# Transposing DMAs for the second LayerNorm's rows, and a lead of three jobs, in a one-core transformer block

## The chip, the cores and the metric

The kernel runs on one core of a Trainium2 chip. A core has a matrix engine (PE), which multiplies into PSUM (eight banks of 512 fp32 columns), a vector engine (DVE), a scalar engine for activations (ACT), a general engine (POOL), and a sync engine (SP), which here issues every DMA. The engines run independent instruction streams and wait for each other by semaphores. The time is device microseconds of one execution; a result is the median over several.

## What is computed

One pre-LayerNorm block on 2048 rows of 1024 bf16 values, with 32 heads of 32 and an FFN of width 3584:

```
x  = A_x
qkv = layernorm(x) @ wqkv
p   = softmax(q k^T * 32**-0.5)          # per head, all 2048 keys, no mask
h   = x + (p v) @ wo
h2  = h + gelu(layernorm(h) @ w1 + b1) @ w2 + b2     # gelu in its tanh form
```

## The kernel before, in words

**Work units.** Rows are cut into 8 units of 256 rows (`UNITS`, line 463), heads into G = 8 groups of 4. A job (unit, group) takes 8 rounds, each of two chunks of 128 keys. A round (`Att.qk`, line 926) is 8 small score matmuls into four PSUM banks (two of the three pairs in banks 0 to 5) and two exps on ACT of 128x1024 each into a slot of the ring PT (9 slots; line 952). `Job.pv` (line 988) multiplies the exps by V and adds up the softmax's denominators: usually DVE adds the round's two chunks into PS (line 1013), for QUAD jobs also two such sums into one (line 1019), and PE multiplies the sums by ones (`den`, line 1029, matmuls at line 1036). The last round of a job is summed "directly" by PE from PT, without DVE. 64 jobs make 1024 exps. `finish` (line 1044) divides and writes OT.

**The lead** (lines 1252 to 1304). Rows are loaded in tiles of 128 (`x_tile`) with slices of the QKV weights (`load_w`), normalized on DVE with a power on POOL (`layer_norm`, line 717; statistics at line 715, the normalization at line 741), transposed by PE through PSUM (line 763), and copied to xnT by ACT (line 770; the ten tiles of `LEAD_ACT`) or DVE (line 772). For each half-chunk hc of 256 rows, `proj_half` (line 898) makes K and, for hc 0 and 1, Q of group 0. As K arrives, rounds of the jobs (0, 0) and (1, 0) start; the exps of the first lie in PT, those of the second in eight buffers PX that overlay K and V of later groups. V of group 0 (`proj_v1`, line 885) follows, then the PVs of the lead's jobs.

**After the lead.** `ORDER` (line 1280) lists first the jobs (2, 0) and (3, 0), then units 0 and 1 for the groups 1 to 7, with the projections of each group just ahead. Q for later units is projected later (`late_q`) by way of a scratch in HBM. From there on, unit by unit: `wo` (line 1099) adds the attention's projection to x, giving hch; `ln2` (line 1139) normalizes hch into xb, and for every unit but the last calls `transposes` (line 760): eight PE transposes into one background bank and one DVE copy into hnT. `ffn1` (line 1162) reads hnT; its first matmul waits for the FFN2 of the unit before. `gelu` runs on DVE with a tanh on ACT (line 1215), and `ffn2` (line 1229) ends the unit. All of this fills PE between the scores and PVs of the attention of units 2 to 7. The last unit's wo, LayerNorm and FFN (`tail=True`) come after all attention and use all banks; its transposes use `transposes_2`.

**What sets the order.** Every operation is a task of a graph (`Graph.add`, line 85) with the buffers it reads and writes, an estimated cost and a priority. `Graph.schedule` (line 110) simulates the engines with these estimates: when an engine comes free, DVE, ACT, POOL and SP take the ready task of least priority number, PE what `pick_pe` (line 1417) chooses among scores, PV, denominators and background work. The order found is written out as fixed instruction streams, so on the chip every engine works strictly in that order. A DMA is modelled as 1.6 us, plus bytes at 340 GB/s, plus 1.0 us, 0.42 us apart on SP, and the large ones (512 KB and over) are also paced. The tables `PV_BEGIN`, `PV_MUST`, `GROUP_SHIFT` and `PRIO_SHIFT` shift that order by numbers found by search. Background matmul groups use banks 6 and 7 only, as does each job's PV.

Of the kernel before, what the change touches and what calls it, by code (L numbers as in the profile page):

```python
# [12 lines left out]
P = 128  # L13
BF = dt.bfloat16
F32 = dt.float32
# [46 lines left out]
class Graph:  # L62
# [47 lines left out]
    def schedule(self, pick_pe, pool, switch=(0.11, 0.106, 0.1), dma_rate=340.0, dma_first=1.6, dma_tail=1.0, dma_issue=0.42,  # L110
# [32 lines left out]
        while n < total:  # L143
# [5 lines left out]
            for e in self.ENGS:  # L149
                while free[e] <= now + 1e-9:  # L150
# [6 lines left out]
                    if e == E.SP and now < state["pace"] - 1e-9:  # L157
                        rs = [x for x in rd if x.bytes < pace_bytes]
                        t = min(rs, key=lambda x: (x.prio, num[x]), default=None)
                        heapq.heappush(events, state["pace"])  # L160
                    elif e == E.PE:
                        t = pick_pe(rd, now, state, free_banks(now))
                    else:
                        t = min(rd, key=lambda x: (x.prio, num[x]))
                        if up and t.prio > 0:

                            for (rt, _, u) in up[:6]:
                                if u.prio < t.prio and rt < now + 0.6 * t.occ:
                                    t = None
                                    break  # L170
# [159 lines left out]
    def emit(self, e, obj):  # L330
# [10 lines left out]
PV_BEGIN = "6887668783765478677666734877585674766834855865775635885656674536"  # L341
PV_MUST = "2563656375427345237632753323452322425663763553734473555222232667"
GROUP_SHIFT = (
# [14 lines left out]
PRIO_SHIFT = (  # L358
# [91 lines left out]
def build_kernel(nc, A_x, A_wqkv, A_wo, B_w1, B_b1, B_w2, B_b2, out):  # L450
# [91 lines left out]

    NS = 3
    ot_lo = Area(top.cur)
    PS, B_PS = sb(top, "PS", [P, NS, 4, 256], BF, NS)
    NOT = 2 * G + 2
    OT, B_OT = sb(top, "OT", [P, NOT, 256], BF, NOT, 2)

# [985 lines left out]
```

## Time and profile before

| | |
|---|---|
| runs | 1078.71, 1082.22 and 5466.11 us; median 1082.22 |
| profiled execution | 1079.89 us |
| its span, first to last instruction | 1078.0 us |
| DMA | 173.93 MB; q1 busy 53.1% of 16 engines' span |
| exps to PT (line 952) | 1008, 937.4 us busy |
| PE transposes for hnT (line 763) | 112, 8.8 us busy |
| DVE copies to hnT (line 772) | 14, 9.4 us busy |
| PS additions (lines 1013, 1019) | 439 in 297.4 us; 191 in 130.8 us |

The first page of the profile gives busy time per engine. PEld is PE's loading of weights beside its matmuls. The rows of tenths cut the span into 40 slices of 27 us; 9 is 90% busy or more. A wait row reads: engine, tile and line that waited, what it waited for, then us in total, times, longest us. A windows row gives a stretch, its length, each engine's busy us (instructions), the granted PE clock, the DMA share and GB/s. A timeline row gives start, length, engine, line, operation, output<-input with shapes; lengths overlap a little, so the pitch from start to start is what an instruction costs its engine. A row of DMA issues ends with its count, KB each and the median us from issue to landing.

### The profile page before, as it was taken

How to read it: one execution, taken by the hardware profiler on the slowest of the kernel's cores; microseconds unless marked ns; L12 is line 12 of the kernel's file. 1: busy time of each engine (PE TensorE's matmuls, PEld its weight loads, DVE VectorE, ACT ScalarE, POOL GpSimd, SP SyncE). 2: the span in 40 equal slices, each digit the busy share in tenths (PEclk: the TensorE clock that was granted, in tenths of full speed). 3: DMA queues.
4: the chain of work that ended last, by engine and by line, in shares of the span. 5: the costliest groups of instructions: out<-in, count | busy, mean ns of one | idle time of the engine just before them, and what ended most of it. 6: DMA issues, size and time to landing. Idle time of an engine off the chain costs nothing.

```text
span 1078.0 us, 38343 instructions
## 1 busy us (share of the span) xinstructions
PE 1037.0 (96%) x17162; PEld 586.8 (54%) x17162; DVE 887.6 (82%) x1737; ACT 1016.2 (94%) x1121; POOL 18.8 (2%) x35
## 2 busy tenths in 40 slices
PE   7889999999999999999999999999999999999998
PEld 5546555554446645654466457456645644564483
DVE  8888677777789997998789979988997997997711
ACT  4999999999999999999999999999999999999850
POOL 2000000000000000000000000000000000000000
DMA  7910010005656575754686667558575755987640
GB/s 196 256 60 3 13 49 2 2 2 175 205 153 204 149 224 167 220 164 132 222 259 183 189 197 203 163 173 260 150 222 184 210 150 162 290 258 236 192 153 20
DMA packets 265492, 173.93 MB, mean 161 GB/s; under 512 B 26864, under 2 KB 259952, under 8 KB 264944
## 3 DMA queue, kind: packets, MB, share of 16 engines
q1 hardware_dynamic: 265328, 171.48, 53.1%
q8 instruction: 135, 2.21, 0.8%
q14 instruction: 29, 0.24, 0.1%
HBM read 161.09 MB, written 10.35 MB: 159 GB/s over the span
## 4 chain that ended last, share of the span: by engine, by line
ACT 85%; PE 10%; DVE 3%; DMA 2%; issue 0%; SPq 0%; DVEq 0%
ACT PT L952 79%; PE ps L672 5%; ACT tg L1215 4%; PE ps L669 3%; ACT PX L952 1%; PE ps L941 1%; DMA a_w1r<-in_B_w_dram 1%; DVE st L715 1%; ACT xnT L770 1%; DMA xrb<-in_A_x_dram 0%; PE ps L996 0%; DVE PS L1013 0%; DMA a_w1r<-in_A_wo_dram 0%; DVE xb L741 0%; DVE gT L1192 0%
## 5 line engine op out<-in xcount | busy, mean ns | idle before, releaser
L952 ACT ACTIVATE PT<-ps 128x1024 bf16<-128x1024 f32 x1008 | 937.4, 1148 | 5.4 <-PE ps L941 5.2
L1013 DVE TENSOR_TENSOR PS<-PT 128x1024 bf16<-128x1024 bf16 x439 | 297.4, 684 | 78.1 <-ACT PT L952 52.1
L941 PE MATMUL ps<-QT,KT 32*128 32x256 bf16 x4096 | 203.6, 273 | 13.6 <-ACT PT L952 9.9
L996 PE MATMUL ps<-PT,V 128*32 128x256 bf16 x4032 | 160.5, 273 | 2.9 <-DVE gT L1192 1.1
L941 PEld LDWEIGHTS ps<-QT,KT 32*128 32x128 bf16 x4096 | 60.8, 92 | 170.0 <-ACT PT L952 157.8
L669 PE MATMUL ps<-hnT,a_w1r 128*128 128x256 bf16 x1197 | 148.1, 273 | 1.8 <-DMA a_w1r<-in_B_w_dram 0.7
L1019 DVE TENSOR_TENSOR PS<-PS 128x1024 bf16<-128x1024 bf16 x191 | 130.8, 685 | 3.4
L669 PE MATMUL ps<-a_w2r,gT 128*128 128x512 bf16 x510 | 125.7, 380 | 3.7 <-DVE hnT L772 1.2
L669 PEld LDWEIGHTS ps<-hnT,a_w1r 128*128 128x128 bf16 x1197 | 109.2, 98 | 35.3 <-issue 20.3
L996 PEld LDWEIGHTS ps<-PT,V 128*32 128x32 bf16 x4032 | 100.9, 96 | 37.5 <-issue 6.3
L666 PE MATMUL ps<-a_w2r,gT 128*32 128x512 bf16 x1096 | 80.2, 382 | 0.4 <-DVE gT L1192 0.2
L669 PEld LDWEIGHTS ps<-a_w2r,gT 128*128 128x128 bf16 x510 | 43.8, 98 | 61.9 <-issue 15.0
L1036 PE MATMUL ps<-PS,ones 128*32 128x256 bf16 x1020 | 70.5, 274 | 0.8 <-DVE PS L1013 0.5
L1192 DVE TENSOR_TENSOR gT<-ps,b1f 128x512 bf16<-128x512 f32 x98 | 66.7, 684 | 4.8 <-PE ps L669 2.4
L666 PE MATMUL ps<-hnT,a_w1r 128*32 128x256 bf16 x1484 | 54.5, 274 | 1.7 <-DMA a_w1r<-in_B_w_dram 0.6
L1215 ACT ACTIVATE tg<-tg 128x1024 bf16<-128x1024 bf16 x49 | 55.6, 1148 | 0.0
L669 PE MATMUL ps<-xnT,Wall 128*128 128x512 bf16 (+1 forms) x241 | 51.9, 345 | 2.5 <-ACT xnT L770 1.6
L669 PE MATMUL ps<-Wall,xnT 128*128 128x256 bf16 x345 | 45.6, 274 | 1.4 <-DVE KT L819 0.8
L666 PEld LDWEIGHTS ps<-hnT,a_w1r 128*32 128x32 bf16 x1484 | 36.3, 96 | 13.4 <-issue 11.2
L666 PE MATMUL ps<-xnT,Wall 128*32 128x512 bf16 x540 | 39.1, 381 | 0.6 <-DVE KT L819 0.6
L1244 DVE SCALAR_TENSOR_TENSOR b_ost<-ps,hch 128x512 bf16<-128x512 f32 x4 | 2.8, 692 | 44.7 <-PE ps L672 44.7
L669 PEld LDWEIGHTS ps<-Wall,xnT 128*128 128x128 bf16 x345 | 31.2, 98 | 12.7 <-issue 5.1
(101 smaller groups left out, 998.0 us busy)
## 6 DMA issues: line engine op xcount, KB each, us to landing
a_w2r<-in_B_w_dram SPq DMA_DIRECT2D x105, 512.0 KB, 4.8
a_w1r<-in_B_w_dram SPq DMA_DIRECT2D x98, 512.0 KB, 4.8
a_w1r<-in_A_wo_dram SPq DMA_DIRECT2D x32, 512.0 KB, 4.5
b_w1r<-in_B_w_dram SPq DMA_DIRECT2D x14, 512.0 KB, 5.0
a_w1r<-in_A_wqkv_dram SPq DMA_DIRECT2D x11, 512.0 KB, 4.0
xrb<-in_A_x_dram SPq DMA_DIRECT2D x16, 256.0 KB, 4.1
Wall<-in_A_wqkv_dram SPq DMA_DIRECT2D x16, 256.0 KB, 4.6
hch<-in_A_x_dram SPq DMA_DIRECT2D x16, 256.0 KB, 4.4
```

The source lines that it names most:

```text
L666: fns.append(lambda p, j=j: p.matmul(psum[32 * j:32 * j + 32, bi(bank), c0:c1], lhsT[:, 32 * j:32 * j + 32], rhs, start=start, stop=stop, ...
L669: t.whole = lambda p: p.matmul(psum[:, bi(bank), c0:c1], lhsT, rhs, start=start, stop=stop, skip_group_check=True)
L672: t = pe(lambda p: p.matmul(psum[:, bi(bank), c0:c1], lhsT, rhs, start=start, stop=stop), occ, reads=reads, writes=[bb(bank)], mode="full" ...
L715: return dve(lambda v: v.bn_stats(st_l[:, i, 6 * c:6 * c + 6], src), 0.6, reads=[B_src], writes=[B_stl[i][c]], prio=prio)
L941: return p.matmul(psum[:, 2 * us[h // 2] + h % 2, n * i:n * i + n], KT[32 * h:32 * h + 32, g, k0:k0 + P], QT[32 * h:32 * h + 32, qs, 0:n], ...
L952: act(lambda a, u=u, k=k: a.activation(pt(s)[:, k, :, :], psum[:, 2 * u:2 * u + 2, :], ACT.Exp, bias=0.0, scale=SCALE), 1024, reads=[B_ps[ ...
L996: fns.append(lambda p, i=i, h=h: p.matmul(psum[32 * h:32 * h + 32, bi(bank), 0:nq], V[:, g, nk * r + i, 32 * h:32 * h + 32], pt(s)[:, h // ...
L1013: dve(lambda v: v.tensor_tensor(PS[:, n, :, :], pairs[:, :, 0:256], pairs[:, :, 256:512], ALU.add), c_dve(1024, 2), reads=[B_PT[2 * s], B_ ...
L1019: dve(lambda v: v.tensor_tensor(PS[:, n, :, :], PS[:, n, :, :], PS[:, m, :, :], ALU.add), c_dve(1024, 2), reads=[B_PS[n], B_PS[m]], writes ...
L1036: fns.append(lambda p, h=h, rhs=rhs, i=i: p.matmul(psum[32 * h:32 * h + 32, bi(bank), nq:2 * nq], ones32[:, :], rhs, start=False, stop=las ...
L1192: drop(dve(lambda v: v.tensor_tensor(gT[:, fc:fc + 2, cs], psum[:, bi(bank), 0:2 * n].rearrange("p (f c) -> p f c", f=2), b1f[:, fc:fc + 2 ...
L1215: act(lambda a: a.activation(t, t, ACT.Tanh, bias=0.0, scale=math.sqrt(2.0 / math.pi)), c, reads=B_t, writes=B_t, prio=-1)
```

## The change

The text of the kernel changes in five places, and the four tables and the two costs of PE's mode switches in the planner are replaced.

1. **Second LayerNorm.** `ln2`, for all units but the last, no longer calls `transposes`; it issues one transposing DMA per tile on SP, from xb to hnT, both in SBUF. The planner charges it as 500000 bytes (it moves 262144), below the size that is paced.
2. **Lead.** It holds three whole jobs, (0, 0), (1, 0) and (2, 0). PX grows from 8 to 14 buffers. The first tile is loaded in two halves; K comes before Q in each half-chunk; K, and Q of the first half-chunk, are projected in pieces of 128 rows; the first Q, K and tiles 0 to 3 use fixed banks; tiles 0 to 3 are normalized one by one at higher priority, and until 16 us of planned time DVE may hold back for a more urgent task that is about to be ready. `LEAD_ACT` keeps tiles 0 to 3. The first V eviction, and K and Q of half-chunk 1, go to ACT. Warm-up matmuls go from 50 to 34.
3. **Sums.** The three lead jobs sum all their rounds directly on PE (`DIRECT` 16). `QA` 6: units 6 and 7 no longer make the second DVE addition.
4. **Order of jobs.** (3, 0), then units 0 to 3 for group 1, units 0 and 1 for groups 2 to 4, then unit 0 for groups 5 to 7 and unit 1 for them. OT gets two more slots.
5. **Planner's costs of weight slices** of 128 columns: 2.4 bytes per element in place of 2, and 3.9 for the first ones.

```diff
-                        if up and t.prio > 0:
+                        if up and (t.prio > 0 or e == E.DVE and now < LEAD_HOLD):
...
-                                if u.prio < t.prio and rt < now + 0.6 * t.occ:
+                                if u.prio < t.prio and rt < now + (0.6 if t.prio > 0 else 0.4) * t.occ:
...
-    for k in range(8):
-        lo = att_lo + 2 * S * (k + 2 if k < 6 else G + k - 2)
+    px_at = [att_lo + 2 * S * a for g in range(1, 5) for a in (g, G + g)] + [att_lo + 2 * S * a for a in (5, 6, 7, G + 5)]
+    px_at += [top.cur + 2 * D * 4, top.cur + 2 * D * 6]
+    for k, lo in enumerate(px_at):
...
-    def dma(out_ap, in_ap, nbytes, reads=(), writes=(), prio=0, noncontig=False, after=()):
+    def dma(out_ap, in_ap, nbytes, reads=(), writes=(), prio=0, noncontig=False, after=(), flip=False):
         def fn(s):
+            if flip:
+                return s.dma_start_transpose(out_ap, in_ap)
...
-    N_WARM = 50
-    LEAD_ACT = [0, 1, 2, 3, 4, 6, 8, 10, 12, 14]
+    N_WARM = 34
+    LEAD_ACT = [0, 1, 2, 3]
...
-    QA = 8
+    QA = 6
...
     def DIRECT(qb, g):
-        return 0 if qb < DA else 1
+        return 16 if g == 0 and qb < DLEAD else 1
...
             else:
-                transposes(R.xb[s][:, :], R.B_xb[s], slot(), hnT[:, :, t * P:(t + 1) * P], B_hnT[t], "dve", 0)
+                dma(hnT[:, :, t * P:(t + 1) * P], R.xb[s][:, :], 500000, reads=[R.B_xb[s]], writes=B_hnT[t], prio=-1, flip=True)
...
-    x_tile(0, -6)
+    x_tile(0, -6, 2)
+    x_tile(1, -6)
     load_w(WQ, -5, 0, P)
-    x_tile(1, -5)
+    x_tile(2, -5)
     load_w(WK, -5, 0, P)
-    x_tile(2, -5)
-    x_tile(3, -5)
-    for tt in range(4, 8):
+    for tt in range(3, 8):
         x_tile(tt, -5)
...
-            tr_tile(tt, slot(), "act" if tt in LEAD_ACT else "dve", ev_prio=-4)
-            if tt + 8 < NT:
-                last_x.append(x_tile(tt + 8, -4))
+            tr_tile(tt, 4 + tt % 2 if hc < LEAD_45 else slot(), "act" if tt in LEAD_ACT else "dve", ev_prio=-4)
+            if hc < 4:
+                last_x.append(x_tile(tt + (12 if hc < 2 else 4), -4))
...
-    ORDER = [(2, 0), (3, 0)] + [(k, g) for g in range(1, G) for k in range(2)]
+    ORDER = [(3, 0)] + [(k, g) for g in range(1, G - LATE) for k in (range(4) if g < NEX else range(2))]
+    ORDER += [(k, g) for k in range(2) for g in range(G - LATE, G)]
...
-        for k, r in {0: [(0, 0)], 1: [(0, 1), (1, 0), (1, 1)]}.get(hc, [(0, hc), (1, hc)]):
-            lead.append((k, r, att.qk((k, 0), r, NR + r if k else None)))
+        for k, r in {0: [(0, 0)], 1: [(0, 1), (1, 0), (1, 1)], 2: [(0, 2), (1, 2), (2, 0), (2, 1), (2, 2)]}.get(hc, [(0, hc), (1, hc), (2, hc)]):
+            if (k, r) != (2, 7):
+                lead[k, r] = att.qk((k, 0), r, None if k == 0 else NR + r if k == 1 else NR + 8 + r if r < 6 else NR - 1)
...
     for hc in range(8):
-        proj_v1(2 * hc, 0, 2, slot(), "dve")
+        proj_v1(2 * hc, 0, 2, slot(), "act" if hc < V_ACT else "dve")
...
-    for k in range(2):
+    for k in range(3):
         job = Job(k, 0, slot(2))
-        for k_, r, s in lead:
-            if k_ == k:
-                job.pv(r, s)
+        for r in range(job.nr):
+            job.pv(r, lead[k, r])
+        if k == 0:
+            lead[2, 7] = att.qk((2, 0), 7)
...
-    gr.schedule(pick_pe, pool_banks, (0.114476, 0.110146, 0.1))
+    gr.schedule(pick_pe, pool_banks, (0.115349, 0.111367, 0.1))
```

The new constants are LEAD_HOLD = 16.0, LEAD_45 = 2, LATE = 3, DLEAD = 3, NEX = 2 and V_ACT = 1.

More of the change, by code (lines that the diff above doesn't have):

```diff
@@ L14 @@
 BF = dt.bfloat16
+LEAD_HOLD = 16.0
+LEAD_45 = 2
+LATE = 3
+DLEAD = 3
+NEX = 2
+V_ACT = 1
 F32 = dt.float32
@@ L338, in emit @@
                 ins.then_inc(self.sems[t.flow], 16 if e == E.SP else 1)
-PV_BEGIN = "6887668783765478677666734877585674766834855865775635885656674536"
-PV_MUST = "2563656375427345237632753323452322425663763553734473555222232667"
+PV_BEGIN = "7577886548677765858856674434636846646566545566645345783555878553"
+PV_MUST = "4534436267554436543436636337557333354424733246352322524333334446"
 GROUP_SHIFT = (
[14 rows of a table removed]
-PRIO_SHIFT = (
[85 rows of a table removed]
[12 rows of a table added]
+PRIO_SHIFT = (
[73 rows of a table added]
 def table(s):
@@ L531, in build_kernel @@
     pt_hi = top.cur
+    NS = 3
     PX, B_PX = [], []
-    for k in range(8):
-        lo = att_lo + 2 * S * (k + 2 if k < 6 else G + k - 2)
+    px_at = [att_lo + 2 * S * a for g in range(1, 5) for a in (g, G + g)] + [att_lo + 2 * S * a for a in (5, 6, 7, G + 5)]
+    px_at += [top.cur + 2 * D * 4, top.cur + 2 * D * 6]
+    for k, lo in enumerate(px_at):
         h_, b_ = sb(Area(lo), "PX%d" % k, [P, 2, 2, 512], BF, 2)
@@ L541, in pt @@
         return PT[:, s, :, :, :] if s < NR else PX[s - NR][:, :, :, :]
-    NS = 3
     ot_lo = Area(top.cur)
+    assert top.cur == px_at[-1] - 2 * D * 6
     PS, B_PS = sb(top, "PS", [P, NS, 4, 256], BF, NS)
-    NOT = 2 * G + 2
+    NOT = 2 * G + 2 * NEX
     OT, B_OT = sb(top, "OT", [P, NOT, 256], BF, NOT, 2)
     def ot(u, g):
-        return 2 * G + u - 2 if g == 0 and u in (2, 3) else u % 2 * G + g
+        return 2 * G + 2 * g + u - 2 if g < NEX and u in (2, 3) else 2 * g + u % 2
     xrb, B_xrb_ = sb(ot_lo, "xrb", [P, 8, D], BF, 16)
@@ L780, in load_w, with x_tile @@
         dma(Wall[:, wp(blk), :, c0:c1], A_wqkv[:, blk * 512 + c0:blk * 512 + c1].rearrange("(dc p) c -> p dc c", p=P),
-            P * DC * (c1 - c0) * 2, writes=B_W[wp(blk)][c0 // P:c1 // P], prio=prio, after=after)
+            P * DC * (c1 - c0) * (2 if c1 - c0 > P else 3.9 if prio == -5 else 2.4), writes=B_W[wp(blk)][c0 // P:c1 // P], prio=prio, after=after)
     def x_slot(tt):
-        return xrb[:, tt % 8, :], B_xrb[tt % 8]
-    def x_tile(tt, prio):
+        i = tt if tt < 8 else tt % 8 ^ 4
+        return xrb[:, i, :], B_xrb[i]
+    def x_tile(tt, prio, parts=1):
         ap, b = x_slot(tt)
-        return dma(ap, x2[tt * P:(tt + 1) * P, :], P * D * 2, writes=b, prio=prio)
+        n = D // parts
+        for i in range(parts):
+            t = dma(ap[:, n * i:n * i + n], x2[tt * P:(tt + 1) * P, n * i:n * i + n], P * n * 2,
+                    writes=b if parts == 1 else [b[i]], prio=prio)
+        return t
     def ln_tiles(tts, prio, norm, quick=True):
         layer_norm([x_slot(tt) + (xb[:, tt % NXB, :], B_xb[tt % NXB]) for tt in tts], prio, norm, quick)
-    N_WARM = 50
-    LEAD_ACT = [0, 1, 2, 3, 4, 6, 8, 10, 12, 14]
+    N_WARM = 34
+    LEAD_ACT = [0, 1, 2, 3]
     def tr_tile(tt, bank, evac, prio=0, ev_prio=0):
@@ L889, in proj_v1 @@
             for dc in range(DC):
-                mm(bank, xnT[:, tc, dc, t4 * P:(t4 + 1) * P], Wall[:, wp(4), dc, P * g:P * g + P], dc == 0, dc == DC - 1,
-                   [B_W[wp(4)][g], B_xnTt[tc][t4]], False, cols=(P * k, P * k + P))
+                m = mm(bank, xnT[:, tc, dc, t4 * P:(t4 + 1) * P], Wall[:, wp(4), dc, P * g:P * g + P], dc == 0, dc == DC - 1,
+                   [B_W[wp(4)][g], B_xnTt[tc][t4]] + ([B_xnTt[tc][i] for i in range(t4, t4 + n)] if k == 0 and dc == 0 else []), False,
+                   cols=(P * k, P * k + P), after=lead_end if g == 1 and k == 0 and dc == 0 else ())
         dst = V[:, g, tt:tt + n, :]
         wr = [B_V[NT * g + tt + k] for k in range(n)]
-        t = dve(lambda v: v.tensor_copy(dst, psum[:, bi(bank), 0:P * n].rearrange("p (t c) -> p t c", t=n)), c_dve_ps(P * n),
-                reads=[bb(bank)], writes=wr, prio=-4 if g == 0 else 0)
+        if evac == "act":
+            t = act(lambda a: a.activation(dst, psum[:, bi(bank), 0:P * n].rearrange("p (t c) -> p t c", t=n), ACT.Copy), P * n,
+                    reads=[bb(bank)], writes=wr, prio=-1)
+        else:
+            t = dve(lambda v: v.tensor_copy(dst, psum[:, bi(bank), 0:P * n].rearrange("p (t c) -> p t c", t=n)), c_dve_ps(P * n),
+                    reads=[bb(bank)], writes=wr, prio=-4 if g == 0 else 0)
         drop(t, bank)
@@ L901, in proj_half @@
         blk = 2 * which
-        for dc in range(DC):
-            mm(bank, Wall[:, wp(blk), dc, 0:P], xnT[:, tc, dc, 256 * h:256 * h + 256], dc == 0, dc == DC - 1,
-               [B_W[wp(blk)][0]] + B_xnTt[tc][2 * h:2 * h + 2], True, cols=(0, 256))
+        n = P if hc == 0 or which == 1 else 256
+        for c in range(0, 256, n):
+            for dc in range(DC):
+                mm(bank, Wall[:, wp(blk), dc, 0:P], xnT[:, tc, dc, 256 * h + c:256 * h + c + n], dc == 0, dc == DC - 1,
+                   [B_W[wp(blk)][0]] + B_xnTt[tc][2 * h + c // P:2 * h + (c + n) // P], n > P, cols=(c, c + n))
         if which == 1:
@@ L912, in proj_half @@
         else:
-            t = dve(lambda v: v.tensor_copy(dst, psum[:, bi(bank), 0:256]), c_dve_ps(256), reads=[bb(bank)], writes=wr, prio=-4)
+            t = dve(lambda v: v.tensor_copy(dst, psum[:, bi(bank), 0:256]), c_dve_ps(256), reads=[bb(bank)], writes=wr, prio=-10 if hc < 2 else -4)
         drop(t, bank)
@@ L922, in __init__ @@
             self.n_units = 3
+            self.pairs = 0
             self.rounds = 0
@@ L932, in qk @@
             nk = 512 // n
-            us = [self.unit % self.n_units, (self.unit + 1) % self.n_units]
-            self.unit += 2
+            if self.pairs:
+                self.pairs -= 1
+                us = [0, 1]
+                self.unit = 2
+            else:
+                us = [self.unit % self.n_units, (self.unit + 1) % self.n_units]
+                self.unit += 2
             fns, banks = [], []
@@ L1261, in build_kernel @@
     for k in range(N_WARM):
-        pe(lambda p: p.matmul(psum[:, 4, 0:256], ident[:, :], b2t[:, 0:256], start=True, stop=True), 0.153,
-           reads=[B_ident, B_b2t], writes=[B_ps[4]], kind="warm")
+        pe(lambda p: p.matmul(psum[:, 3, 0:256], ident[:, :], b2t[:, 0:256], start=True, stop=True), 0.153,
+           reads=[B_ident, B_b2t], writes=[B_ps[3]], kind="warm")
     def lead_norm(hc):
         tts = [2 * hc, 2 * hc + 1]
-        if hc == 0:
-            ln_tiles(tts[:1], -6, "dve", True)
-            ln_tiles(tts[1:], -5, "dve", True)
+        if hc < 2:
+            for tt in tts:
+                ln_tiles([tt], tt - 12, "dve", True)
         else:
@@ L1278, in lead_norm @@
             dma(xd[tc - 1], xnT[:, tc, :, :], P * 8192, reads=B_xnTt[tc], writes=[B_xd[tc - 1]], prio=1)
-    ORDER = [(2, 0), (3, 0)] + [(k, g) for g in range(1, G) for k in range(2)]
+    ORDER = [(3, 0)] + [(k, g) for g in range(1, G - LATE) for k in (range(4) if g < NEX else range(2))]
+    ORDER += [(k, g) for k in range(2) for g in range(G - LATE, G)]
     made = []
     last_x = []
-    lead = []
+    lead = {}
+    lead_end = []
     lead_norm(0)
     for hc in range(8):
-        ev = "act" if hc == 0 else "dve"
-        if hc < 2:
+        ev = "act" if hc < 2 else "dve"
+        if hc == 0:
+            proj_half(0, 0, 0, ev)
+        proj_half(1, hc, slot() if hc else 1, ev)
+        if 0 < hc < 3:
             proj_half(0, hc, slot(), ev)
-        proj_half(1, hc, slot(), ev)
         if hc < 7:
             lead_norm(hc + 1)
-        for k, r in {0: [(0, 0)], 1: [(0, 1), (1, 0), (1, 1)]}.get(hc, [(0, hc), (1, hc)]):
-            lead.append((k, r, att.qk((k, 0), r, NR + r if k else None)))
-    if ORDER[0] == (2, 0):
-        proj(0, 0, 1, slot(), "dve", direct=True)
-        made.append(0)
+        for k, r in {0: [(0, 0)], 1: [(0, 1), (1, 0), (1, 1)], 2: [(0, 2), (1, 2), (2, 0), (2, 1), (2, 2)]}.get(hc, [(0, hc), (1, hc), (2, hc)]):
+            if (k, r) != (2, 7):
+                lead[k, r] = att.qk((k, 0), r, None if k == 0 else NR + r if k == 1 else NR + 8 + r if r < 6 else NR - 1)
+    att.rounds = NR
+    proj_half(0, 3, slot(), "dve")
+    made.append(0)
     for hc in range(8):
-        proj_v1(2 * hc, 0, 2, slot(), "dve")
+        proj_v1(2 * hc, 0, 2, slot(), "act" if hc < V_ACT else "dve")
+    lead_end.append([t for t in gr.tasks if t.eng == E.PE and t.kind == "bg"][-1])
     pv_last += [t for t in gr.tasks if t.eng == E.PE and t.kind == "bg"]
-    for k in range(2):
+    for k in range(3):
         job = Job(k, 0, slot(2))
-        for k_, r, s in lead:
-            if k_ == k:
-                job.pv(r, s)
+        for r in range(job.nr):
+            job.pv(r, lead[k, r])
+        if k == 0:
+            lead[2, 7] = att.qk((2, 0), 7)
     N_LEAD = 0
@@ L1332, in rest_of_projections @@
             proj(1, g, tc, slot(), "dve")
+        if g < NEX:
+            made.append(g)
+            proj(0, g, 1, slot(), "dve", direct=True)
         if g == 1:
@@ L1366, in build_kernel @@
     ffn1(0)
-    attention(2, [g for g in range(G) if (2, g) not in ORDER])
+    attention(2, [g for g in range(1, G) if (2, g) not in ORDER])
     for u in range(NU - 3):
```

184 rows, old and new, of tables (GROUP_SHIFT, PRIO_SHIFT) are left out of this document.

## Prediction

> **What bounds the kernel now.** I read the page's busy shares and slices first, to see which engine is full and where it is not; then ACT's waits; then windows over the stages; then the timeline around a second LayerNorm; last the DMA issues, for the price of the new transfer.
>
> ```profile
> PE 1037.0 (96%) x17162; PEld 586.8 (54%) x17162; DVE 887.6 (82%) x1737; ACT 1016.2 (94%) x1121; POOL 18.8 (2%) x35
> DVE  8888677777789997998789979988997997997711
> ACT  4999999999999999999999999999999999999850
> ```
>
> ACT is full from the second slice to the last three. PE's 96% is not a bound by itself, as its ends are modelled.
>
> ```profile
> ACT xnT L770 <- PE ps L763: 11.0, 3, 8.9
> ACT gT L1198 <- PE ps L672: 8.7, 12, 0.8
> ACT PT L952 <- PE ps L941: 5.2, 10, 1.0
> ```
>
> The last line: exps wait for scores only 5.2 us in all. Everything else that ACT loses lies before its first exps or in the last unit's FFN.
>
> ```profile
> core 0: us, PE busy (x) PEld busy (x) DVE busy (x) ACT busy (x) POOL busy (x), PEclk, DMA share, GB/s
> 18.00:24.00 6.00, 4.41 (x57) 3.29 (x56) 6.00 (x21) 3.57 (x4) 1.38 (x2) 1.00 0.40 130
> 24.00:52.00 28.00, 23.75 (x323) 15.56 (x322) 25.66 (x69) 27.98 (x31) 2.76 (x4) 1.00 0.92 236
> 60.00:230.00 170.00, 163.88 (x2919) 92.03 (x2915) 134.40 (x243) 169.95 (x187) 0.00 (x0) 1.00 0.04 12
> 770.00:1010.00 240.00, 231.05 (x3945) 125.31 (x3943) 214.03 (x409) 238.75 (x260) 2.58 (x4) 1.00 0.70 209
> ```
>
> By stage: up to 24 us DVE is the full engine (6.00 of 6.00) and ACT starves; from 24 us on ACT is full. So the time is ACT's work from 24 us to the last exp near 1018, plus the tail. Only three things pay: ACT starting earlier, ACT having less to do, or a shorter tail. Taking work from DVE or PE in the middle pays at most the few us that ACT idles there.
>
> **The change, part by part.** The sum is made against the profiled execution: 1079.9 us, span 1078.0. The median of the runs shown is 1082.2, 0.2% above it.
>
> *Evictions in the lead.* LEAD_ACT shrinks from ten tiles to four. ACT's pitch for a 1024-column instruction is 0.92 us (170.65 us for 186 in the chain). After the first exp at 17.69, ACT now evicts seven tiles (3, 4, 6, 8, 10, 12, 14): 6.4 us. Afterwards about one (0.92), and it gains K and Q of the second half-chunk and one V, 256 columns, 0.30 each: 1.8 in all. Gain 4.6 us. DVE takes six more copies at 0.68, 4.1 us, in 24 to 52 us, where it has 2.3 us free and loses seven additions of the lead's jobs (4.8 us), which start at 42.55 in its timeline. The copies come earlier than that; what covers them is the third job: a half-chunk of K now feeds three rounds, 3 x 2 x 0.92 = 5.5 us of exps, no longer 3.7. Without that cover ACT would lose up to the 4.1 us.
>
> *The start.* ACT becomes continuous at 24.02, when K of the second half-chunk is there. DVE runs without a gap from 8.11 on, but in its timeline the tiles 2 and 3 wait behind statistics of tiles 4 to 6 four times (about 0.5, 0.6, 0.5, 0.6 us) and behind a V copy (0.35): 2.5 us. Then PE does Q, a V projection and two groups of transposes ahead of K: at least 1 us. The new priorities, K before Q, V put last and the split first load remove these. Bounds 0 and 5 us; I take 3.5. That V is put last costs at the lead's exit, below.
>
> *Lead's exit.* V's eight projections (1.24 us each by the timeline) and 24 rounds of PV, no longer 16, stand in line there, and K of group 1 lies where two of the lead's rounds are kept, so it waits for their PV. While ACT works off nine rounds (16.6 us), PE needs about 9 rounds of PV with direct sums (0.88 each), 8 scores (0.44 each) and five projections of 1.73: 20 us. ACT may starve 0 to 3.5 us; I take 1.7, the middle, as the order can slide some of it. No row shows this place.
>
> *Sums.* The three lead jobs sum on PE, all 16 chunks: 30 DVE additions of 0.68 go (20 us), 120 narrow matmuls come. Units 6 and 7 drop the second addition: 48 x 0.68 = 33 us off DVE, 192 matmuls more on PE. A run of them goes at 0.0275 us each, a lone group of four shows 0.069: 3.3 to 8 us and 5.3 to 13.3 us. The DVE time is worth nothing by itself where ACT is full. Those two units' exps fill about 770 to 1018 us (16 jobs x 16 x 0.92 and the tanhs between). PE has 8.9 us of room in 770 to 1010, and is spared four tiles' transposes there (2.5 us): cost 0 to 1.9 us, I take 0. If that cover is gone, PV comes late, next the PT buffers, then ACT.
>
> *The transposes.* For 14 row tiles go: eight PE transposes (0.62 us, 8.7 in all), one DVE copy (0.68, 9.5 in all) and a bank. 14 DMA issues come to SP's 431; at 0.38 us each 5 us of SP. Each waits for the normalized rows, and behind it wait SP's next loads, mostly weights, which run several blocks ahead. No row shows a transposing DMA, so from both sides:
>
> ```profile
> hch<-in_A_x_dram SPq DMA_DIRECT2D x16, 256.0 KB, 4.4
> b1b<-in_B_b_dram SPq DMA_DIRECT2D x1, 7.0 KB, 8.5
> out_dram<-b_ost SPq DMA_DIRECT2D x4, 128.0 KB, 1.7
> ```
>
> The floor is 1.7 us; the same bytes in long rows take 4.4. The ceiling is b1b: 3584 pieces of 2 bytes in 8.5 us, so 131072 pieces would take some 300 us. I take 4.4, the row with the same bytes and the same 2 KB rows at one end. What may it cost? From the end of the second tile's normalization to the first matmul on hnT, units 0 to 6 now take 18.1, 7.9, 23.1, 8.6, 15.0, 17.4 and 5.1 us. The shortest:
>
> ```profile
> 921.68 0.55 DVE L741 TENSOR_SCALAR a_xb<-hch,mvr,rden 128x1024 bf16<-128x1024 bf16 x1
> 926.61 0.64 DVE L772 COPY hnT<-ps 128x1024 bf16<-128x1024 bf16 x1
> 927.31 0.28 PE L669 MATMUL ps<-hnT,a_w1r 128*128 128x256 bf16 x1
> ```
>
> At 4.4 us no unit is later than before, and FFN2 of the unit before fills PE meanwhile: cost nothing, and no gain, as ACT is full. If late, PE stands, and ACT runs on for the scores in six banks, 3 x 0.92 = 2.75 us.
>
> The Trainium skill bears on this. "VectorE: DVE Perf Modes", The three transpose paths, speaks against the change: 390 ns for a 128x128 transpose on TensorE, 1309 ns by the DMA crossbar, and TensorE where PSUM will do; eight in a row would be an estimated 10.5 us, and the sum by it 1076 with the gaps of before, or 1099 if the new order leaves each unit only the 4.1 us that its planner charges. "Advanced Engine Details and Errata", X-Bar Transpose (TRN2), says that they are as fast as ordinary DMAs, which gives the sum below. No run so far shows either.
>
> *Orders and the rest.* The tables re-order everything; in the middle ACT can gain at most its 5 us of idle time, and I take 0. Sixteen fewer warm-up matmuls end before the first tile is there, at no cost.
>
> Sum: 1079.9 - 4.6 - 3.5 + 1.7 = **1073.5 us**.
>
> **The rivals.**
>
> *Transposes land late (slower).* PE's queue is in order: an FFN1 that waits also holds the scores behind it, so ACT starves. With landing time L the loss is the sum over units of L - gap - 2.75 where positive. With the gaps of before: 6 us at L = 12, 28 at 19, 32 at 20; with only the planner's 4.1 us in all seven units, 7 x (L - 6.85): 28 at 10.9. Past 1101.5 us from L = 11 to 19 on. For it: 2-byte pieces are dear (b1b), and SP may be held as long. Against: the row of equal bytes. Time 1102 to 1140, far more if it moves element by element. The Trainium skill's 1309 ns, in the section named above, is the rule of this kind; its estimated 10.5 us would stand just short of that edge.
>
> *PE becomes the bound.* At the lead's exit (1.8 more than taken) and in units 6 and 7 (1.9, and as much as 8 if switches between shapes double the sums' price there), with the start's gain missing (3.5): 1080 to 1087. For it: PE at 163.88 of 170. Against: transposes leave PE.
>
> *More is gained.* The start gives 1.5 more, the lead's exit costs nothing (1.7), the middle's 5 go, and a shorter DVE chain before the tail gives up to the 3.4 us that ACT waits there for statistics: 1061.9; 1058 to 1064. For it: DVE is 60 us lighter. Against: ACT is full nearly everywhere.
>
> *The transposes change nothing* is part of my forecast: all its gain is in the lead.
>
> **How the numbers follow.** Forecast (1064 to 1080) 0.62; PE bound 0.16; late transposes 0.17; more gained 0.05. The range leaves out the last and most of the late case: 1064 to 1105. Two per cent, about what a measurement of this kernel can tell from no change, are 1058.3 and 1101.5. Faster by more: 0.02, the edge of the last case. Slower by more: 0.18, the late case and a little of PE's. Within: 0.80.
>
> **What would show it.** Right: exps without a gap from about 20.5 us on; xnT copies on ACT four times; a transposing issue lands in 3 to 7 us; ACT's wait for scores stays under 10 us. Wrong: PE waits for a DMA into hnT with ACT idle behind it, SP issues far over 0.5 us, or gaps in the exps between 60 and 85 us or in 770 to 1010.

## The result and the profile after

The changed kernel takes 1075.1 us (median of six runs, 1071.4 to 1075.6), the kernel before 1081.6 in the same comparison: a ratio of 0.993, interval 0.9916 to 0.9944, 6 to 9 us less. The profiled execution, 1071.4 us with a span of 1069.6, is the fastest of the six; against the profiled one of before the span is 8.4 us shorter.

The page and ACT's waits, of the changed kernel:

```profile
PE 1028.5 (96%) x18417; PEld 593.4 (55%) x18469; DVE 836.2 (78%) x1654; ACT 1012.3 (95%) x1118; POOL 19.1 (2%) x36
...
DVE  8857877777799997999699979979984986796611
ACT  5999999999999999999999999999999999999850
```

```profile
ACT xnT L766 <- PE ps L759: 8.1, 2, 6.9
...
ACT PT L966 <- PE ps L955: 3.9, 8, 0.7
```

DVE lost 51 us, PE 8.5 and ACT only 3.9. ACT's share stays the same, because the span shrank with it. The wait for the first tile (the first row, its longest) fell from 8.9 to 6.9 us; the wait for scores (the last row) was 5.2 and is 3.9. The page's chain of work that ended last ran 85% over ACT and 10% over PE before; now it runs 70% over ACT and 24% over PE. PE has come closer to being the limit, which the experiments take up.

The windows that answer to those shown before (the last one shifted, as the exps now end near 1009 us):

```profile
core 0: us, PE busy (x) PEld busy (x) DVE busy (x) ACT busy (x) POOL busy (x), PEclk, DMA share, GB/s
18.00:24.00 6.00, 5.46 (x88) 4.10 (x86) 4.86 (x15) 5.09 (x7) 0.69 (x1) 1.00 0.75 231
24.00:52.00 28.00, 23.70 (x347) 16.17 (x347) 24.46 (x69) 27.05 (x30) 3.02 (x4) 0.94 0.88 218
60.00:230.00 170.00, 166.93 (x3224) 100.25 (x3224) 127.08 (x233) 169.45 (x186) 0.00 (x0) 1.00 0.06 19
760.00:1005.00 245.00, 238.05 (x4528) 133.64 (x4541) 186.63 (x363) 243.32 (x265) 2.72 (x4) 1.00 0.75 217
```

In 18 to 24 us DVE is no longer full (4.86 of 6.00) and ACT works 5.09 us where it worked 3.57. The granted clock in 24 to 52 us is 0.94, where it was 1.00; no run here shows what that costs. ACT alone in the first 24 us, before and after:

```profile
0.00:24.00 24.00, 8.89 (x10) 1.00 0.74 198
```

```profile
0.00:24.00 24.00, 13.24 (x17) 1.00 0.80 209
```

Splitting the whole span into ACT's work and its idle time accounts for all 8.4 us:

| ACT, profiled executions | before | after | difference |
|---|---|---|---|
| idle, 0 to 24 us | 15.1 | 10.8 | -4.3 |
| idle, 24 to 60 us | 0.5 | 0.9 | +0.5 |
| idle, 60 us to about 5 us before the last exp ends (1013, 1005) | 4.0 | 2.8 | -1.1 |
| idle from there to the end | 42.3 | 42.7 | +0.4 |
| work, whole span | 1016.2 | 1012.3 | -3.9 |

So the profile puts the gain into the lead: ACT starts earlier, and has less to do. The medians differ by 6.5 us and these two executions by 8.4; the table can't say in which row the other 2 us lie. The start in the timeline of ACT, before and after:

```profile
24.02 1.02 ACT L952 ACTIVATE PT<-ps 128x1024 bf16<-128x1024 f32 x1 [1.00 <-PE ps L941]
```

```profile
19.29 1.02 ACT L966 ACTIVATE PT<-ps 128x1024 bf16<-128x1024 f32 x1 [0.61 <-PE ps L955]
20.21 0.38 ACT L919 ACTIVATE QT<-ps 128x256 bf16<-128x256 f32 x1
20.48 1.03 ACT L966 ACTIVATE PT<-ps 128x1024 bf16<-128x1024 f32 x1
21.38 3.80 ACT L966 ACTIVATE PX<-ps 128x1024 bf16<-128x1024 f32 x4
```

From 19.29 us on ACT runs on, but for 0.20 us at 36 and 0.66 us at 46, where it did from 24.02.

The new transfer, in the view of the tile hnT (lengths in ns: least, median, most) and among the DMA issues:

```profile
L683 SPq DMA_TRANSPOSE hnT<-a_xb x14: 1237/1320/2577, 306.4 to 915.4; - x14
...
DMA to landing us min/median/max: 2.7/4.9/7.4
```

```profile
hch<-in_A_x_dram SPq DMA_DIRECT2D x16, 256.0 KB, 4.1
...
hnT<-a_xb SPq DMA_TRANSPOSE x14, 4.9
```

It lands about like a plain load of its size (4.9 against 4.1 us), but it holds SP for 1.3 us, three times the 0.4 that most loads take.

### The profile page after: what moved, and what is told of

Its sections match the earlier page's. It is cut to its first block, busy times and chain, and to the rows that moved or that the text cites. A ratio compares the mean times of both kernels' runs of the same rounds, so it can differ in the third digit from the quotient of the medians.

```text
span 1069.6 us, 40833 instructions
## 1 busy us (share of the span) xinstructions
PE 1028.5 (96%) x18417; PEld 593.4 (55%) x18469; DVE 836.2 (78%) x1654; ACT 1012.3 (95%) x1118; POOL 19.1 (2%) x36
## 3 DMA queue, kind: packets, MB, share of 16 engines
q1 hardware_dynamic: 279824, 174.89, 56.5%
## 4 chain that ended last, share of the span: by engine, by line
ACT 70%; PE 24%; DVE 3%; DMA 2%; issue 0%; POOL 0%; POOLq 0%; SPq 0%
ACT PT L966 66%; PE ps L663 6%; PE ps L666 6%; PE ps L660 5%; PE ps L955 3%; ACT tg L1229 3%; PE ps L1010 2%; PE ps L1050 1%; DMA a_w1r<-in_B_w_dram 1%; DVE PS L1027 1%; DVE st L711 1%; DMA hnT<-a_xb 1%; PE ps L1275 1%; DMA q_scratch<-a_ost 0%; DVE xnT L768 0%
## 5 line engine op out<-in xcount | busy, mean ns | idle before, releaser
L966 ACT ACTIVATE PT<-ps 128x1024 bf16<-128x1024 f32 x996 | 924.4, 1140 | 4.1 <-PE ps L955 3.9
L955 PE MATMUL ps<-QT,KT 32*128 32x256 bf16 x4096 | 204.0, 273 | 10.1 <-ACT PT L966 4.9
L663 PE MATMUL ps<-hnT,a_w1r 128*128 128x256 bf16 x1030 | 126.8, 273 | 3.9 <-DVE gT L1206 1.4
L663 PEld LDWEIGHTS ps<-hnT,a_w1r 128*128 128x128 bf16 x1030 | 94.1, 98 | 32.2 <-issue 18.4
L660 PE MATMUL ps<-a_w2r,gT 128*32 128x512 bf16 x1560 | 110.0, 381 | 1.4 <-DVE OD L1085 1.0
L1033 DVE TENSOR_TENSOR PS<-PS 128x1024 bf16<-128x1024 bf16 x135 | 92.6, 686 | 2.5
L663 PE MATMUL ps<-a_w2r,gT 128*128 128x512 bf16 x367 | 89.7, 380 | 4.4 <-issue 2.7
L660 PE MATMUL ps<-hnT,a_w1r 128*32 128x256 bf16 x2152 | 77.6, 274 | 3.2 <-DVE gT L1206 0.9
L660 PEld LDWEIGHTS ps<-hnT,a_w1r 128*32 128x32 bf16 x2152 | 52.2, 96 | 19.7 <-issue 16.0
L660 PEld LDWEIGHTS ps<-a_w2r,gT 128*32 128x32 bf16 x1560 | 34.8, 96 | 30.7 <-issue 16.0
L1050 PEld LDWEIGHTS ps<-PS,ones 128*32 128x32 bf16 x1160 | 30.9, 96 | 16.6 <-issue 5.3
```

The lines of the kernel that those rows point to most:

```text
L660: fns.append(lambda p, j=j: p.matmul(psum[32 * j:32 * j + 32, bi(bank), c0:c1], lhsT[:, 32 * j:32 * j + 32], rhs, start=start, stop=stop, ...
L663: t.whole = lambda p: p.matmul(psum[:, bi(bank), c0:c1], lhsT, rhs, start=start, stop=stop, skip_group_check=True)
L955: return p.matmul(psum[:, 2 * us[h // 2] + h % 2, n * i:n * i + n], KT[32 * h:32 * h + 32, g, k0:k0 + P], QT[32 * h:32 * h + 32, qs, 0:n], ...
L966: act(lambda a, u=u, k=k: a.activation(pt(s)[:, k, :, :], psum[:, 2 * u:2 * u + 2, :], ACT.Exp, bias=0.0, scale=SCALE), 1024, reads=[B_ps[ ...
L1033: dve(lambda v: v.tensor_tensor(PS[:, n, :, :], PS[:, n, :, :], PS[:, m, :, :], ALU.add), c_dve(1024, 2), reads=[B_PS[n], B_PS[m]], writes ...
L1050: fns.append(lambda p, h=h, rhs=rhs, i=i: p.matmul(psum[32 * h:32 * h + 32, bi(bank), nq:2 * nq], ones32[:, :], rhs, start=False, stop=las ...
```

## The experiments

Two theories at the start. *Lead*: the whole gain is in the lead, ACT is the bound, and the transposing DMAs only have to land in time. *Relief*: the gain is the work that the transposes took off PE and DVE. In the first eight kernels the order of every engine is that of their base; only what is issued in a place changes. All ratios are to the kernel before, on the same chip. The experiments ran on several chips, on which the kernel before took 1081.6 to 1082.6 us; differences in us from the changed kernel are of medians, and by the ratios they come out up to 1.1 us greater.

**e1, plain copies in place of transposes.**

```diff
-                return s.dma_start_transpose(out_ap, in_ap)
+                return s.dma_start(out_ap, in_ap.rearrange("p (d c) -> p d c", d=DC))
```

> The changed kernel with the same order of all engines, but its 14 transposing DMAs are plain copies of the same 256 KB from xb to hnT (nothing is transposed, so the FFN of units 0 to 6 reads untransposed rows). Lead theory (all of the gain is in the lead, and the transposes land in time): 1075 us, within 1.5 us of the changed kernel, although SP is held for about 0.4 us in place of 1.3 per issue. Rival (the transposing form itself costs, by SP's time or by the DMA engines' time): 2 to 6 us faster, 1069 to 1073.

Measured: 1075.7 us, ratio 0.9928 (0.9907 to 0.9950), the same as the changed kernel's. The DMA issues of this run and its view of the tile:

```profile
hnT<-a_xb SPq DMA_DIRECT2D x14, 256.0 KB, 4.6
```

```profile
L683 SPq DMA_DIRECT2D hnT<-a_xb x14: 594/606/1214, 306.0 to 916.3; - x14
```

A plain copy of the same bytes holds SP half as long and lands 0.3 us sooner, and the median doesn't move. The transposing form costs nothing here that this run can tell; its six times lie between 1072.1 and 1078.0 us, so a cost of 1 or 2 us isn't excluded.

**e2, every transpose twice, one after the other.** Ahead of each transposing DMA SP issues a copy of it; the second waits until the first has landed. `N_EXTRA` is 1.

```diff
+        if t.kind == "flip":
+            for k in range(N_EXTRA):
+                x = Task(E.SP, t.fns, t.occ, t.lat, 0, "", None)
+                x.deps = set(t.deps)
...
+                seq.append(x)
+                gr.tasks.append(x)
+                t.deps.add(x)
+        seq.append(t)
```

> The changed kernel with every transposing DMA issued twice, the second after the first has landed; all other orders unchanged. The second tile of a unit then lands some 10 us later (twice 4.9 us). Between the landing and the first matmul on hnT the changed kernel's trace has about 6, 13, 29, 10, 10, 20 and 0 us in units 0 to 6, and ACT runs on for 2.75 us. Lead theory with late transposes costing only what exceeds that: units 0 and 6 lose 1 and 7 us, 1081 to 1086 us in all. Rival (SP is held while it waits, so weights come late everywhere): 1090 us or more. Second rival (all lateness is absorbed): 1075 to 1077.

Measured: 1107.4 us, ratio 1.0233 (1.0211 to 1.0255): 32 us more than the changed kernel, beyond the lead theory's 6 to 11. ACT's wait for scores, SP's wait for the first copies, and two of PE's waits:

```profile
ACT PT L967 <- PE ps L956: 35.7, 27, 8.7
```

```profile
SPq L684 <- DMA hnT<-a_xb: 41.1, 14, 5.4
```

```profile
PE ps L664 <- DMA hnT<-a_xb: 7.6, 1, 7.6
...
PE ps L664 <- DMA a_w2r<-in_B_w_dram: 4.0, 2, 3.7
```

ACT's row grew by 31.8 us, which is nearly the whole loss. SP stood 2.9 us per tile, beside one more issue of 1.25. PE waited for hnT itself only once, in unit 6. By the trace's landing times a unit's second tile came 4 to 7 us later after its normalization than in the changed kernel, not 10. Where the rest of the loss arises is seen in the chain of unit 1, which had 13 us to spare between landing and first use (the pieces of "issue" between the rows, 0.02 to 0.04 us each, are left out):

```profile
404.28 5.65 DMA hnT<-a_xb
409.95 1.78 SPq L684
411.78 2.00 DMA out_dram<-a_ost
413.80 0.70 DVE a_ost L1259
414.55 1.08 PE ps L661 x16
```

Behind the waiting SP stood a store of a result tile; the tile's buffer (two exist) came free late, so DVE's next eviction waited, so PE's next group had no bank, so the scores behind it in PE's queue were late. Unit 0's chain has the same form, with a store of Q to its scratch. In unit 5's chain it was a weight load that stood behind the waiting SP, and PE waited 3.7 us for it:

```profile
811.31 7.29 DMA hnT<-a_xb
...
819.95 4.65 DMA a_w2r<-in_B_w_dram
```

Unit 0 lost 4.1 us in 300 to 330 and unit 5 5.6 in 790 to 830; in unit 6, with no time to spare, ACT stood 8.7 us at once. The rival, that SP is held and what stands behind it comes late, is right in the units 0 to 5, for stores as for weights; in unit 6 hnT itself is late.

The stalls also lowered the clock. PE stood 2.8, 2.9, 3.7 and 7.6 us in units 0, 1, 5 and 6, and right after each of these waits the granted clock fell. PE alone before and after the end of the wait in unit 5:

```profile
821.00:825.00 4.00, 0.36 (x5) 1.00 1.00 224
825.00:829.00 4.00, 4.00 (x25) 0.57 1.09 378
```

In the other three the clock is 0.57, 0.57 and 0.52 over the 4, 4 and 7 us that follow; the changed kernel has 1.00 in all four places.

**e3, ACT's saved work put back.** Six lead exps run twice: what is put into `again` is issued again right behind itself.

```diff
+                if (qb, g) == (1, 0) and 3 <= r < 6:
+                    again.add(t)
```

> The changed kernel with six exps of the lead's second job done twice (ACT gets 6 x 0.92 us and a wait of about 0.15 us each more, the amount that the six moved evictions took from it); all orders unchanged. Lead theory (ACT is the bound from the lead on, so its work counts one for one): 1080 to 1082 us. Rival (PE or DVE is the bound by now, and ACT's work hardly counts): 1075 to 1077.

Measured: 1080.9 us, ratio 0.9987 (0.9972 to 1.0002), 5.8 us more than the changed kernel for 5.5 us of exps and six short waits, with a spread of 1078.1 to 1085.2 us. ACT's work in the lead counts one for one.

**e4, e5 and e6, dummies on PE and DVE.** e4 has both, e5 PE's alone (the first three lines below), e6 DVE's alone (the normalization, the last two).

```diff
+                        if f == 0 and dc == 0 and not tail:
+                            t = ffn1_end[u]
+                            t.fns, t.whole = t.fns + t.fns, lambda p, w=t.whole: (w(p), w(p))[1]
...
+            if twice:
+                again.add(t)
```

> The changed kernel with the work that the transposes took off PE and DVE put back as dummies: the normalization of each of the 14 tiles runs twice on DVE (0.5 us each and a wait), and the first matmul of every first half of an FFN1 block of units 0 to 6 runs twice on PE (14 x 7 x 0.11 to 0.13 us, 11 to 13 us in all); all orders unchanged. Lead theory (that relief is worth nothing, as ACT is full): 1075 to 1077 us. Rival (the relief is what was gained): 1081 to 1088.

> The changed kernel with only the dummies on PE (the first matmul of every first half of an FFN1 block of units 0 to 6 runs twice, 98 matmuls of 0.11 to 0.13 us); all orders unchanged. If PE's lack of room made the loss of the run with both dummies: 1079 to 1082 us. If DVE's dummies did (they also let the transposing DMAs start later): 1075 to 1076.5.

> The changed kernel with only the dummies on DVE (the normalization of the 14 tiles runs twice, 0.5 us and a wait each); all orders unchanged. If PE's lack of room made the loss of the run with both: 1075 to 1076.5 us. If DVE did: 1079 to 1082.

Measured: e4 1081.9 us, ratio 0.9993 (0.9979 to 1.0008); e5 1080.8, 0.9990 (0.9977 to 1.0003); e6 1076.7, 0.9955 (0.9938 to 0.9971). DVE's dummies cost 1.6 us by the medians and 2.7 by the ratios, little more than the spread. PE's cost 6, more than half of the 8.6 us by which PE's busy time grew. The lead theory as I had put it, that PE's work in the middle is worth nothing, fails in this direction. ACT's wait for scores doesn't tell the two apart: it is 8.2 us in e5 and 7.6 in e6. The chain that ended last does; in e5 PE's share of it is 42%, in e6 the 24% of the changed kernel:

```profile
ACT 50%; PE 42%; DMA 4%; DVE 3%; issue 1%; SPq 0%
```

```profile
ACT 65%; PE 24%; DVE 6%; DMA 4%; issue 1%; POOL 0%; SPq 0%; DVEq 0%; POOLq 0%
```

**e7, the kernel before, transposes left out for units 1 to 6** (the edit: seven of eight PE transposes of a tile are not issued, and the copy takes one block).

> The kernel before with the order of all engines unchanged, but units 1 to 6 carry out only the last of a tile's eight transposes and copy only that block (the other blocks of hnT stay those of unit 0, so the FFN of units 1 to 6 reads wrong rows): 12 x 0.54 us less on PE, 12 x about 0.5 us less on DVE, with nothing in their place. Lead theory (in the kernel before that relief is worth nothing): 0.998 to 1.002 of the kernel before. Relief theory: 0.994 to 0.997, 3 to 6 us less.

Measured: 1084.2 us, ratio 1.0017 (1.0006 to 1.0028). The work is gone (PE 1026.3 us busy, was 1037.0), and the time is no shorter; it is even 2 us longer, for a reason that isn't shown. A lower clock doesn't hide a gain: the two of its runs with a granted clock of 1.00 took 1083.3 and 1083.8 us, against the 1082.3 of the kernel before. Taken alone, with the order as it is, the relief shows no worth.

**e8, PE's dummies in the kernel before** (the edit of e5).

> The kernel before with the same dummies on PE as the run with only PE's (98 matmuls twice); all orders unchanged. If the order of the kernel before is as tight on PE as the changed one: 1.003 to 1.006 of it, 4 to 7 us more. If it has room that the changed kernel used up (sums moved from DVE to PE in the lead and in units 6 and 7): 1.000 to 1.002.

Measured: 1089.8 us, ratio 1.0072 (1.0049 to 1.0095), 7.5 us more, a little above the range given. So the kernel before was as tight on PE as the changed one; the changed one has not used up room that was there.

**e9 to e12, a square.** e7 leaves open that a new order could use the room. A kernel whose transposes are put back can't be compared under tables made for the other, so all four start from empty tables (`GROUP_SHIFT`, `PRIO_SHIFT`, flat `PV_BEGIN` and `PV_MUST`) and got new ones by the same small search on the planner's own model. Between the columns the edit is the one line of `ln2`; between the rows it is everything else of the diff.

> First of four kernels in a square: the lead, sums and job order of the kernel before or of the changed one, by transposes on PE or by DMA. All four start from empty order tables and were searched anew on the planner's own model with the same small effort, so that none has tables that fit another. This one: old lead, transposes on PE (the kernel before with new tables). 1080 to 1088 us.

> Square: old lead, transposes by DMA. Lead theory (the transposes give nothing even when the order may use the room): within 2 us of old lead with PE transposes. Rival (the order uses PE's and DVE's room): 4 to 7 us below it.

> Square: new lead, sums and job order, transposes on PE. Lead theory: 6 to 8 us below old lead with PE transposes (about what the whole change measured). Rival: 0 to 4 us below it.

> Square: new lead, transposes by DMA (the changed kernel with new tables). Lead theory: within 2 us of new lead with PE transposes. Rival: 4 to 7 us below it. Either way 1070 to 1078 us.

| us, ratio (interval) | transposes on PE | by DMA |
|---|---|---|
| old lead, sums, job order | 1092.7, 1.0090 (1.0069 to 1.0110) | 1096.1, 1.0122 (1.0102 to 1.0142) |
| new | 1081.5, 0.9993 (0.9980 to 1.0006) | 1079.6, 0.9987 (0.9969 to 1.0005) |

The lead with its sums and job order is worth 11 us with the transposes on PE and 16 by DMA. In the traces, ACT idles 6.6 us less before 300 us from e9 to e11 and 4.4 less from e10 to e12, and it works 5.4 and 3.7 us less; together 12.0 us where the spans differ by 10.1, and 8.1 where they differ by 8.4. The transposes take 3.4 us more with the old lead and 1.9 less with the new; the rival's 4 to 7 us less shows in neither row. But new tables alone move the time by 4 us (e12 against the changed kernel) and 10 (e9 against the one before), so the square can't resolve a few us: that the transposes give nothing where the order is free is shown only to that coarseness. Misses: e9 and e12 came out above the ranges given, e10 lies 3.4 us above e9 where at most 2 were expected, and e11 11 us below e9 where 6 to 8 were. So the old lead lives on its tables more than the new one, and a size can't be carried over from this square, only which edge of it moves the time more. It isn't isolated further which of the new lead, the direct sums and the job order carries it; the table of ACT's idle time points at the first.

## Why the prediction was right

*Evictions, 4.6 us.* ACT's work fell by 3.9 us, and e3 shows that this counts in full. Right in mechanism, 0.7 too much.

*The start, 3.5 us.* ACT's idle time before 24 us fell by 4.3. The size is right, within its bounds, but the reasons given are not the whole. About 2.0 us of it are there at the first eviction, which starts at 8.92 us and did at 10.90: DVE now does the statistics of one other tile ahead of the first tile's normalization, where it did those of two and waited 1.5 us for their loads. And the warm-up matmuls are not free, as I had taken them to be:

```profile
2.42 6.01 PE ps L1275 x33
```

This piece of the changed kernel's chain is the warm-up. By the timeline the first tile is normalized at 7.13 us, and PE begins its transposes only at 8.27, when 33 warm-up matmuls are done. What fewer of them would give isn't shown.

*The lead's exit, 1.7 us lost.* This term was mis-sized; it is zero. In the changed kernel's timeline one run of exps stands from 61 us on:

```profile
61.42 68.99 ACT L966 ACTIVATE PT<-ps 128x1024 bf16<-128x1024 f32 x75
```

75 exps in 68.99 us are 0.92 each, with no gap. What ACT loses lies earlier, 0.9 us within the lead; 0.66 of it, at 46 us, stands behind the tile copies that DVE took over, so the third job covers them but for that. The sum of terms was 6.4 us less than the profiled 1079.9. The profile, against which it was made, shows 8.4 less: besides the lead's exit, ACT's idle time in the middle fell by 1.1, which I had put at nothing. That 6.4 also meets the 6.5 us of the medians is in part luck.

*Sums.* Units 6 and 7 give up 48 additions on DVE (33 us) for 192 more matmuls; I took no cost. ACT's idle time in those units is 1.7 us (245 - 243.32), after 1.3 before. Right.

*The transposes, nothing.* I took 4.4 us to land from the loads of 256 KB; the trace shows 4.9, and e1's plain copy 4.6. With that they are in time for six units, and in unit 6 PE waits 0.65 us:

```profile
921.76 0.81 PE L663 MATMUL ps<-hnT,a_w1r 128*128 128x256 bf16 x6 [0.65 <-DMA hnT<-a_xb]
```

That they bring nothing by themselves is shown by e7 in the old order, and by the square to within a few us. The Trainium skill's page "Advanced Engine Details and Errata", X-Bar Transpose (TRN2), has transposing DMAs as fast as ordinary ones; 4.9 against 4.6 us agree with it. The estimate of 10.5 us from the 1309 ns in the Trainium skill's page "VectorE: DVE Perf Modes", The three transpose paths, does not hold for eight blocks in one DMA: the trace has 4.9 us from issue to landing, 7.4 at most.

*What was wrong though the time was right.* Three steps. SP's price, 0.38 us from the plain issues, is 1.32 in the trace; issues far over 0.5 us stood among my signs of being wrong, and they came without a cost. "PE's 96% is not a bound by itself": it is one in one direction. Taking 10.7 us of busy time from PE gave nothing (e7), adding 8.6 cost 6 (e5). A reading that fits, and that no run tests further: ACT is full only while PE delivers scores just in time; work that leaves PE leaves ACT as the bound, work that comes displaces scores. The late rival's price, the sum of what exceeds each unit's gap, let landing times up to 11 to 19 us pass before 2% is lost. e2 lost 3% with SP held only some 4 us longer per tile; with the changed kernel's gaps and tiles at most 7 us later that price is some 4 us, all in unit 6. I counted what waits for hnT and not what is queued behind the waiting SP: stores whose buffers DVE and PE need, and weights, which I had taken to "run several blocks ahead".

## What to carry to other kernels

Split the span into the bounding engine's work and its idle time, stage by stage, for both kernels: the two differences add up to the change, and show at once which edits can have paid. An engine at 95% beside the bound must be tested in both directions: here less work on it was worth nothing, while more cost over half of its length. A DMA that waits on an in-order queue is priced by what stands behind it; here that was stores with two buffers, and weight loads.

## What the hardware showed that I had not expected

A transposing DMA of 128x1024 bf16 within SBUF holds SP for 1.24 to 2.58 us per issue, a plain copy of the same bytes there 0.59 to 1.21, and a load of 256 KB from HBM about 0.4. That difference doesn't show in the time (e1). The change added packets to the queue (265328 in 171.48 MB before, 279824 in 174.89 MB after) and lifted its share of the DMA engines from 53.1% to 56.5%, with no weight load's median landing more than 0.6 us later. In e2, PE's four waits of 2.8 to 7.6 us were each followed by some us at a granted clock of 0.52 to 0.57, so a late DMA can cost more than the wait itself.
